# An attention and ReGLU kernel: pair 0's k over a hardware DMA queue instead of GpSimd's

## The chip, the cores and the metric

The kernel runs on one core of a Trainium2 chip. The time is the device time of one execution in microseconds (us); for a version of the kernel it is the median of several runs. One further execution is taken by the hardware profiler, and all times inside the kernel are from that one, counted from the start of its span. The engines are TensorE (PE, with its weight loads as PEld), VectorE (DVE), ScalarE (ACT), GpSimd (POOL) and SyncE (SP). DMAs are issued by SP and ACT over hardware queues, and by GpSimd[...]; only GpSimd's DMAs change the type of the data on the way here (fp32 in HBM to fp16 on the chip).

## What is computed

Eight batches of eight heads, 576 positions, 64 values per head. Each head has two attentions: one over positions averaged in fours, whose result is repeated four times, and one in a band of seven positions. Their sum goes through a gated feed-forward network.

```python
q_d = q.reshape(B, H, Sd, factor, D).mean(axis=3)      # k_d, v_d likewise; factor = 4
out_up = np.repeat(sm_attn(q_d, k_d, v_d), factor, axis=2)
mask = np.abs(pos[:, None] - pos[None, :]) < factor
scores = np.where(mask, scale * np.matmul(q, k.transpose(0, 1, 3, 2)), -1e9)
x = out_up + np.matmul(softmax(scores), v)             # to (4608, 512)
out = (np.maximum(x @ w_gate, 0.0) * (x @ w_val)) @ w_out
```

## The kernel before

The 64 heads are worked off as 32 pairs. For each pair, q, k and v are loaded as fp16 with positions on the partitions: q and k as 96 x 12 x 64 in one slot of a ring of seven (`qk16`), v as 112 x 12 x 64 (`vw`). Then q and k are transposed, so that the 64 values of a head lie on the partitions; pairs from 9 on have this done by DMA transposes and have q and k loaded in two halves each, while the first nine pairs are "flipped" by PE: `emit_flip` (L358) multiplies blocks of q and k by a small constant (an identity beside a matrix that sums fours), and ACT or DVE copy the product out of PSUM into `qkT` and `qkd` (`emit_flipped`, L372). After the flips come the scores (`emit_s1_mm`, L422), exponentials on ACT (`emit_exp`, `emit_ed`), the band mask on DVE (`emit_mask`), and the products with v and pooled v (`emit_s2u`, `emit_s2d`). v is pooled by matmuls with another constant (`emit_vd`, L403). The results are collected, transposed, in `xT`; the feed-forward network takes them in nine chunks of 512 tokens (`emit_h_mm`, L636, and the products with w_out), and the attention of later pairs runs between its matmuls.

Nothing here is scheduled by a compiler: every engine and queue executes in the order in which the program emits. The beginning is the list `FRONT` (L18), a sequence of steps written out by hand, from left to right: `loadk/0` loads pair 0's k, `tr/0/2/4` flips the third part of pair 0 into PSUM bank 4, `ev/0/20V/4` copies it out on DVE (`V`; `A` is ACT), `vd/0/6` pools v, `s1/0/2` are scores, `warm/5/6` are five matmuls on zeros which keep PE busy, `pads` are memsets (`emit_pads`, L279) of the parts of `ee`, `ed`, `vd` and `xo` that no later step writes. PE, for instance, meets pair 0's flips in the order 2, 1, 0, then pools pair 0's v, then runs five matmuls on zeros, and then flips part 0 of pair 1 ahead of pair 0's scores. Of pair 0's flips, part 2 needs k alone, part 1 k and q, part 0 q alone.

Ahead of the list stand (L1097 to L1101):

```python
nc.scalar.dma_start(cst_sb[:, 960:1080], cst_dr[:, 960:1080])
emit_load_q1(0, 0)
nc.sync.dma_start(cst_sb[:, 0:960], cst_dr[:, 0:960])
nc.sync.dma_start(cst_sb[:, 1080:1368], cst_dr[:, 1080:1368])
emit_warm(14, wide=True)
```

The constants are masks and pooling weights (0:960), the flip's constant (960:1080) and one for repeating (1080:1368). Pair 0's q is loaded here by SP in fp32 into `q32`, and ACT casts it into its slot (step `cast`, L1055). All other loads of q, k and v are issued by GpSimd (`emit_load_q1` at L296, `emit_load_v` at L314), one after the other in the order of the list: k and v of pair 0, q, k, v of pair 1, and so on, then slices of the weights. GpSimd's DMAs take eight semaphores in turn, so each waits for the one that was issued eight before it. `gT` (L248) holds the gated hidden layer in two buffers; `gT[1]` is first written by the second chunk of the network.

Of the kernel before, what the change touches and what calls it, by code (L numbers as in the profile page):

```python
# [9 lines left out]
FP32 = mybir.dt.float32  # L10
# [5 lines left out]


FRONT = """  # L18
pads loadk/0 loadv/0 loadq/1 loadk/1 loadv/1 loadq/2 cast tr/0/2/4 loadk/2 ev/0/20V/4 tr/0/1/3
tr/0/0/2 ev/0/21V/4 ev/0/10A/3 vd/0/6 loadv/2 ev/0/11A/3 ev/0/01A/2 ev/0/00A/2 loadq/3 warm/5/6  # L20
tr/1/0/7 vc/0/6 s1/0/2 ev/1/00A/7 loadk/3 tr/1/2/1 ed/0/2 tr/1/1/0 ev/1/20V/1 ev/1/11A/0 loadv/3
sd/0/6 ev/1/21V/1 ev/1/10A/0 rd/0/6 ex/0/0/2 td/0/6 wg/0 vd/1/6 ev/1/01A/7 warm/5/7 ma/0/0
ex/0/1/2 s1/1/0 wv/0 ma/0/1 ed/1/0 ones/4 su/0/4 ex/1/1/0 ru/0/4 loadq/4 ex/1/0/0 tu/0/0/4
# [131 lines left out]
def _dap(t_ap: bass.AP, extra_off: int, dims) -> bass.AP:  # L155
    return bass.AP(tensor=t_ap.tensor, offset=t_ap.offset + extra_off, ap=list(dims))
# [13 lines left out]
def kernel(  # L170
# [10 lines left out]
    nc = tc.nc  # L181
    B, H, S, D = q.shape
# [3 lines left out]
    NB = S // NQ  # L186
    SD = S // 4
# [33 lines left out]
    def ring(n, shape, dtype, name):  # L221
        return [keep.tile(shape, dtype, name=f"{name}{i}") for i in range(n)]
# [5 lines left out]
    qk16 = [t[0:96] for t in qkfull]  # L228
# [7 lines left out]
    ee = ring(2, [WK, 2, S + 32], FP16, "ee_")  # L236
    ed = ring(2, [72, 2, 2 * SD + 64], FP16, "ed_")
    vd = ring(3, [72, 2, 192], FP16, "vd_")
# [7 lines left out]
    q32 = q32full[0:96]  # L246
    r1 = ring(3, [128, TCH], FP16, "r1_")
    gT = ring(2, [128, NJJ, TCH], FP16, "gT_")  # L248
    xT = keep.tile([128, NPB, NTOK], FP16, name="xT")
    ps = psum.tile([128, 8, 512], FP32, name="ps")  # L250

# [24 lines left out]
    for t in qkT:  # L276
        nc.vector.memset(t[:, 2 * S :], 0.0)

    def emit_pads():  # L279
        for t in ee:  # L280
            nc.vector.memset(t[:, :, S:], 0.0)
        for t in ed:
            nc.vector.memset(t[:, :, 2 * SD :], 0.0)
        for t in vd:
            nc.vector.memset(t[:, :, 64:128], 4.0)
        for t in xo:
            nc.vector.memset(t[64:96, NB:, :], 0.0)
# [4 lines left out]
    def head_off(hp):  # L292
        b = (hp // NPB + B0) % B
        return b, (b * H + 2 * (hp % NPB)) * S * D

    def emit_load_q1(hp, i):  # L296

        b, off = head_off(hp)
        src, dst, hh = (q, k)[i // 2], qk16[hp % NL][:, i // 2, :], i % 2
        if hp < NTP:  # L300
            if hh:
                return
            first = hp == 0 and src is q
            (nc.sync if first else nc.gpsimd).dma_start(
                (q32 if first else dst).rearrange("p (n d) -> p n d", d=64),
                _dap(src, off, [[D, 96], [NQ * D, 2 * NB], [1, D]]),
            )
            return
        nc.gpsimd.dma_start(  # L309
            dst.rearrange("p (j h d) -> p j h d", h=2, d=64)[:, :, hh, :],  # L310
            _dap(src, off + hh * S * D, [[D, 96], [NQ * D, NB], [1, D]]),
        )
# [497 lines left out]
    def emit_warm(n, bank=7, wide=False):  # L810
        for _ in range(n):
            nc.tensor.matmul(
                out=ps[:, 7, :] if wide else ps[:, bank, 264:512],
                lhsT=zero_sb[:, 0:128],
                rhs=zero_sb[:, 128 : 640 if wide else 376],
                start=True,
                stop=True,
            )
# [114 lines left out]
    def emit_tail_step(kind, arg, at):  # L933
        c, j = (int(at[0]), int(at[1])) if len(at) == 2 else (int(at or 0), 0)
        i = int(arg[0]) if arg else 0
        if kind in ("hg", "hv"):
            w = int(kind == "hv")
            bank = 4 + i if w else 2 * (j % 2) + i
            emit_h_mm(c, j + NK * i, w, range(4), ps[:, bank, :])
        elif kind == "relu":  # L940
            emit_relu(2 * j + i, ps[:, 2 * (j % 2) + i, :])
        elif kind == "gate":
            emit_gate(c, j + NK * i, 2 * j + i, ps[:, 4 + i, :])
        elif kind in ("gateg", "gateb"):
            nc.vector.scalar_tensor_tensor(
                out=gT[c % 2][:, j + NK * i, :],
                in0=block(c, j, 0).t[i],
                scalar=0.0,
                in1=ps[:, 4 + i, :] if kind == "gateg" else block(c, j, 1).t[i],
                op0=ALU.max,  # L950
                op1=ALU.mult,
            )
        elif kind == "xs":
            emit_xs(c, i)
        elif kind == "wg":
            emit_ws(0, i, 0, 768, nc.vector)
        elif kind == "wv":
            emit_ws(1, i, 192 * int(arg[1]), 192 * int(arg[1]) + 192, nc.gpsimd)
        elif kind in ("qg", "qv"):
            block(c, j, int(kind == "qv")).q(i)  # L960
        elif kind in ("keepg", "keepv"):
            block(c, j, int(kind == "keepv")).keep(i - 1)
        elif kind in ("tg", "tv"):
            block(c, j, int(kind == "tv")).out(arg)
        elif kind == "part":
            lo, hi = ((0, 3), (3, 5), (5, 6))[int(arg[1])]
            unit(c, j).sums(lo, hi, (i,))
        else:
            UNIT_STEPS[kind](unit(c, j), i)

    def emit_step(kind, arg, u, c):

        banks = (u, 1 - u)
        i = int(arg[-1]) if arg and arg[-1].isdigit() else 0
        if kind in H_STEPS:
            pp, jj = banks[i % 2], 6 * u + i
            if kind == "relu":
                emit_relu(i, pair(pp)[:, 0, :])
            elif kind == "gate":
                emit_gate(c, jj, i, pair(pp)[:, 1, :])  # L980
            else:
                w = int(kind == "hv")
                emit_h_mm(c, jj, w, range(4), pair(pp)[:, w, :])
        elif kind in UNIT_STEPS:
            UNIT_STEPS[kind](unit(c - 1, u), i)
        elif kind == "next":
            w = unit(c - 1, 1) if u == 0 else unit(c, 0)
            w.sums(0, NK if u == 0 else 5, (i,))
        else:
            PAIR_STEPS[kind](4 * c + 2 * u + LEAD + "ab".index(arg[0]), arg[1:])  # L990
# [22 lines left out]
    def pool_ab(hp, a):  # L1013
# [15 lines left out]
        "v1": lambda hp, a: emit_v1(hp + 1),  # L1029
        "v2": lambda hp, a: emit_v2(hp + 2),  # L1030
        "qk": ahead(emit_load_q1),
        "v": ahead(emit_load_v),
        "v4": ahead(emit_load_v4),
    }

    def emit_periods(c0, c1):
        for base in range(c0, c1 + 2):
            for tok in ORDER.split():
                c = base + {">": 1, "<": -1}.get(tok[-1], 0)
                kind, arg, u = tok.rstrip("<>").split("/")  # L1040
                if c == c1 - 1 and base > c:
                    continue
                if c0 <= c < c1 or c == c0 - 1 and f"{kind}/{arg}/{u}" in LATE:
                    emit_step(kind, arg, int(u), c)

    def emit_front(tok):
        kind, *a = tok.split("/")
        if "@" in tok:
            emit_step(kind, a[0], *map(int, a[1].split("@")))
        else:  # L1050
            FRONT_STEPS[kind](*[int(x) if x.isdigit() else x for x in a])

    FRONT_STEPS = {
        "pads": emit_pads,
        "cast": lambda: nc.scalar.copy(out=qk16[0][:, 0, :], in_=q32),  # L1055
        "warm": emit_warm,
        "loadq": lambda p: emit_load_q1(p, 0),
        "loadk": lambda p: emit_load_q1(p, 2),
        "loadv": emit_load_v,
        "ones": lambda p: nc.gpsimd.memset(vw[p][:, :, 64:128], 1.0),  # L1060
# [34 lines left out]

    with tc.manual_schedule(engines={ET.PE, ET.DVE, ET.Activation, ET.SP, ET.Pool}):
        nc.scalar.dma_start(cst_sb[:, 960:1080], cst_dr[:, 960:1080])  # L1097
        emit_load_q1(0, 0)
        nc.sync.dma_start(cst_sb[:, 0:960], cst_dr[:, 0:960])
        nc.sync.dma_start(cst_sb[:, 1080:1368], cst_dr[:, 1080:1368])  # L1100
        emit_warm(14, wide=True)  # L1101
        for tok in FRONT.split():
            emit_front(tok)
        emit_periods(PS // 4, (NP - LEAD) // 4)
        for tok in TAIL.split():
            kind, arg, *at = tok.split("/")
            if at:
                emit_tail_step(kind, arg, at[0])
            else:
                emit_step(kind, arg, 1, NCH - 3)  # L1110
# [30 lines left out]
```

## Time and profile before

| | |
|---|---|
| median of five runs | 346.85 us (345.49 to 347.64) |
| profiled execution: its own time, its span | 345.49 us, 343.7 us |
| PE busy, share of the span | 336.4 us, 98% |
| DVE, ACT, POOL busy | 296.7, 218.0, 183.0 us |
| granted clock of PE, mean | 0.999 |
| GpSimd's DMA queue | 132160 packets, 22.63 MB |
| hardware DMA queue of SP | 35632 packets, 16.84 MB |
| PE busy from 0 to 8.2 us, from 8.2 to 24.3 us | 6.74 and 14.26 us (with the matmuls on zeros) |
| PE busy from 24.3 to 60 us | 35.41 of 35.70 us |
| longest wait of PE for a DMA | 0.2 us (0.5 of its weight loads), once |

A matmul counts as busy while it is in the pipeline, so 98% does not mean that PE works at its peak. In the lists below, "SPq" and "ACTq" are DMA issues by SP and ACT[...]. "L304" is a line of the kernel above. In square brackets stands how long the engine had been idle, and what ended that.

### The profile page before, as it was taken

The numbers are of one execution on the slowest core, as the hardware profiler recorded it, in microseconds if no ns is written. First come the engines' busy times: TensorE is split into PE (matmuls) and PEld (weight loads), VectorE is DVE, ScalarE is ACT, GpSimd is POOL, SyncE is SP. The second block draws the span as 40 slices with busy tenths as digits, with TensorE's granted clock in tenths as the row PEclk, the third lists the DMA queues.
The fourth block names the chain that finished last, engine by engine and source line by source line (L and its number), as shares of the span: only waits on it lengthen the run. The fifth ranks groups of instructions, "written<-read, shape, count | busy, mean of one in ns | idle before, by whom it ended". The sixth has DMA issues, their size and how long they took to land.

```text
span 343.7 us, 8266 instructions
## 1 busy us (share of the span) xinstructions
PE 336.4 (98%) x3231; PEld 215.8 (63%) x3231; DVE 296.7 (86%) x546; ACT 218.0 (63%) x423; POOL 183.0 (53%) x232
## 2 busy tenths in 40 slices
PE   8899999999999999999999999999999999999996
PEld 4675556656575656575666556665766557768685
DVE  6694779988999999999999999899999798786892
ACT  4878767767767776677667767776677633334222
POOL 8986557776999796989197777840300000000000
PEclk9999999999999999999999999999999999999999
DMA  9999999999999999999999995992100001001023
GB/s 154 167 170 187 186 190 161 143 168 159 173 145 191 138 188 108 137 162 145 109 108 132 148 162 80 151 154 41 46 16 33 31 2 46 32 31 61 28 67 108
DMA packets 167974, 40.02 MB, mean 116 GB/s; under 512 B 149856, under 2 KB 164864, under 8 KB 167936
## 3 DMA queue, kind: packets, MB, share of 16 engines
q0 software_dynamic: 132160, 22.63, 92.7%
q1 hardware_dynamic: 35632, 16.84, 27.1%
q8 instruction: 25, 0.41, 0.5%
q14 instruction: 13, 0.11, 0.1%
q10 hardware_dynamic: 144, 0.03, 0.1%
HBM read 45.86 MB, written 9.44 MB: 161 GB/s over the span
## 4 chain that ended last, share of the span: by engine, by line
PE 88%; ACT 4%; DVE 3%; DMA 2%; issue 1%; POOL 1%; DVEq 0%; ACTq 0%; POOLq 0%
PE ps L639 47%; PE ps L724 22%; PE ps L905 4%; PE ps L585 3%; PE ps L438 2%; PE ps L427 2%; PE ps L593 2%; PE ps L364 1%; DMA qk<-in_q_dram 1%; PE ps L408 1%; DVE xn L612 1%; ACT rden L603 1%; ACT ed L462 1%; ACT ee L448 1%; DVE xo L718 0%
## 5 line engine op out<-in xcount | busy, mean ns | idle before, releaser
L639 PE MATMUL ps<-xT,wv_sb 128*128 128x512 f16 x432 | 109.0, 379 | 0.0
L639 PE MATMUL ps<-xT,wg_sb 128*128 128x512 f16 x352 | 88.4, 380 | 0.0
L648 ACT ACTIVATE r<-ps 128x512 f16<-128x512 f32 x88 | 52.0, 596 | 31.8 <-PE ps L639 28.9
L639 PEld LDWEIGHTS <-wv_sb 128*128 128x128 f16 x432 | 40.4, 98 | 39.7
L651 DVE TENSOR_TENSOR gT<-r,ps 128x512 f16<-128x512 f16 x88 | 58.9, 680 | 7.0 <-PE ps L639 4.1
L639 PEld LDWEIGHTS <-wg_sb 128*128 128x128 f16 x352 | 32.6, 98 | 32.3 <-issue 0.2
L612 DVE TENSOR_TENSOR xn<-ps,rden 64x720 f16<-64x720 f32 x48 | 43.5, 905 | 4.9 <-ACT rden L608 3.5
L603 ACT ACTIVATE rden<-ps 64x720 f32<-64x720 f32 x48 | 36.7, 765 | 14.2 <-PE ps L593 13.2
L448 ACT ACTIVATE ee<-ps 112x576 f16<-112x576 f32 x64 | 38.7, 647 | 6.2 <-PE ps L438 5.2
L309 POOL DMA_DIRECT2D qk<-in_k_dram x46 | 33.7, 738 | 8.2 <-DMA qk<-in_q_dram 3.6
L309 POOL DMA_DIRECT2D qk<-in_q_dram x46 | 33.7, 737 | 7.9 <-DMA qk<-in_k_dram 4.1
L724 PEld LDWEIGHTS <-gT 128*128 128x128 f16 x324 | 31.5, 98 | 9.0
L454 DVE TENSOR_TENSOR ee<-ee,cst_sb 112x576 f16<-112x576 f16 x64 | 31.6, 514 | 5.2 <-ACT ee L448 4.8
L334 POOL DMA_DIRECT2D vw<-in_v_dram x30 | 28.6, 952 | 8.3 <-PE ps L639 4.9
L724 PEld LDWEIGHTS <-xo 128*128 128x128 f16 x288 | 27.4, 98 | 7.7 <-DVE xo L718 0.3
L351 DVE TENSOR_REDUCE qkd<-qkT 128x288 f16<-128x1152 f16 x23 | 30.9, 1343 | 0.0
L758 ACT COPY q<-ps 128x256 f32<-128x256 f32 x45 | 16.8, 372 | 21.5 <-PE ps L724 21.2
L724 PE MATMUL ps<-wo_sb,gT 128*128 128x256 f16 x216 | 28.0, 273 | 0.0
L724 PE MATMUL ps<-wt,xo 128*128 128x256 f16 x216 | 27.7, 273 | 0.2 <-DVE xo L718 0.2
L386 POOL TENSOR_TENSOR v<-v 72x512 f32<-72x512 f16 x21 | 25.7, 1223 | 2.6 <-DMA v<-in_v_dram 2.0
L571 DVE TENSOR_TENSOR xT<-xn 128x576 f16<-128x576 f16 x28 | 24.1, 861 | 0.5
L915 ACT COPY vw<-ps 128x256 f32<-128x256 f32 x30 | 10.8, 374 | 20.7 <-PE ps L905 13.8
(108 smaller groups left out, 557.5 us busy)
## 6 DMA issues: line engine op xcount, KB each, us to landing
out_dram<-y_sb SPq DMA_DIRECT2D x24, 256.0 KB, 3.8
vw<-in_v_dram POOLq DMA_DIRECT2D x30, 168.0 KB, 7.4
qk<-in_q_dram POOLq DMA_DIRECT2D x46, 72.0 KB, 7.0
qk<-in_k_dram POOLq DMA_DIRECT2D x46, 72.0 KB, 6.7
v<-in_v_dram POOLq DMA_DIRECT2D x21, 144.0 KB, 7.3
out_dram<-y_sb SPq DMA_DIRECT2D x22, 128.0 KB, 1.7
wg_sb<-in_moe_w_gate_dram POOLq DMA_DIRECT2D x4, 384.0 KB, 9.6
wv_sb<-in_moe_w_val_dram POOLq DMA_DIRECT2D x4, 384.0 KB, 10.8
```

Of the source, the lines that this page charges most:

```text
L309: nc.gpsimd.dma_start(dst.rearrange("p (j h d) -> p j h d", h=2, d=64)[:, :, hh, :], _dap(src, off + hh * S * D, [[D, 96], [NQ * D, NB], [ ...
L334: nc.gpsimd.dma_start(t, _dap(v, base, [[D, WK], [NQ * D, n], [1, D]]))
L351: nc.vector.tensor_reduce(out=qkd[hp % 2].rearrange("p i t -> p (i t)"), in_=qkT[hp % 4][:, 0 : 2 * S].rearrange("p (t f) -> p t f", f=4), ...
L386: nc.gpsimd.tensor_tensor(out=m, in0=t[:, :, 0:128], in1=t[:, :, 128:256], op=ALU.add)
L448: nc.scalar.activation(out=o, in_=ps[0:WK, p0 + 2 * g : p0 + 2 * g + 2, 0:288], func=AF.Exp, scale=scale)
L454: nc.vector.tensor_tensor(out=o, in0=o, in1=_sap(masks_sb, (0, WK), 288 * g, [[0, 2], [1, 288]]), op=ALU.mult,)
L603: nc.scalar.activation(out=rden[lo : lo + 64], in_=ps[de : de + 64, 4 + 2 * hh : 6 + 2 * hh, 0:360], func=AF.Ln)
L612: nc.vector.tensor_tensor(out=xn[lo : lo + 64], in0=ps[lo : lo + 64, 4 + 2 * hh : 6 + 2 * hh, 0:360], in1=rden[lo : lo + 64], op=ALU.mult,)
L639: nc.tensor.matmul(out=out, lhsT=w[:, kk, bass.ts(jj, 128)], rhs=xT[:, kk, c * TCH : (c + 1) * TCH], start=(kk == 0), stop=(kk == 3),)
L648: nc.scalar.activation(out=r1[j % 3], in_=h1, func=AF.Relu)
L651: nc.vector.tensor_tensor(out=gT[c % 2][:, jj, :], in0=r1[j % 3], in1=h2, op=ALU.mult)
L724: nc.tensor.matmul(out=out, lhsT=left[:, i, :], rhs=right[i], start=(first and i == 0), stop=(i == NK - 1), skip_group_check=True,)
```

## The change

- `emit_load_q1` sends pair 0's k over SP in fp32, into `k32`, which is a view of the still unused `gT[1]`, and pair 0's q over ACT. k is emitted ahead of q: SP issues k, then its two constants; ACT issues its small constant, then q. GpSimd's first DMA is now pair 0's v, and its list is shorter by one.
- A new step `castk` casts `k32` into pair 0's slot on DVE. In DVE's order it stands after the memsets of `ee` and `ed`, ahead of pair 0's first copies.
- `emit_pads` is split: `pads/0` does `ee` and `ed` where `pads` stood; `pads/1` does `vd` and `xo` after the copies `ev/0/20V` and `ev/0/21V`.
- The first run of matmuls on zeros has 11 instead of 14.

In the order of the engines, these are all of the differences: PE has three matmuls (and their weight loads) less, DVE one cast more, and the six memsets of `vd` and `xo` two copies later, ACT one issue more, GpSimd one issue less, and on SP k stands where q stood. Waits that are new: PE's first flip waits for DVE instead of a GpSimd DMA, pair 0's first pooled product waits for DVE too, and single later instructions wait for the new DMA or the new cast (GpSimd's reload of pair 0's k slot, PE's first read of `gT[1]`, one store of SP). Line numbers grow by 1 to 7 in the changed kernel: L304 becomes L309, L364 becomes L369, L378 L383, the cast of q L1061; the new cast is L1060.

```diff
-pads loadk/0 loadv/0 loadq/1 loadk/1 loadv/1 loadq/2 cast tr/0/2/4 loadk/2 ev/0/20V/4 tr/0/1/3
-tr/0/0/2 ev/0/21V/4 ev/0/10A/3 vd/0/6 loadv/2 ev/0/11A/3 ev/0/01A/2 ev/0/00A/2 loadq/3 warm/5/6
+pads/0 castk loadv/0 loadq/1 loadk/1 loadv/1 loadq/2 cast tr/0/2/4 loadk/2 ev/0/20V/4 tr/0/1/3
+tr/0/0/2 ev/0/21V/4 pads/1 ev/0/10A/3 vd/0/6 loadv/2 ev/0/11A/3 ev/0/01A/2 ev/0/00A/2 loadq/3 warm/5/6
...
+    k32 = gT[1].rearrange("p j t -> p (j t)")[0:96, 0 : 4 * NB * 64].bitcast(FP32)
...
-    def emit_pads():
-        for t in ee:
-            nc.vector.memset(t[:, :, S:], 0.0)
-        for t in ed:
-            nc.vector.memset(t[:, :, 2 * SD :], 0.0)
+    def emit_pads(i):
+        if i == 0:
+            for t in ee:
+                nc.vector.memset(t[:, :, S:], 0.0)
+            for t in ed:
+                nc.vector.memset(t[:, :, 2 * SD :], 0.0)
+            return
         for t in vd:
             nc.vector.memset(t[:, :, 64:128], 4.0)
...
-            first = hp == 0 and src is q
-            (nc.sync if first else nc.gpsimd).dma_start(
-                (q32 if first else dst).rearrange("p (n d) -> p n d", d=64),
+            eng = nc.gpsimd
+            if hp == 0:
+                eng, dst = (nc.scalar, q32) if src is q else (nc.sync, k32)
+            eng.dma_start(
+                dst.rearrange("p (n d) -> p n d", d=64),
...
+        "castk": lambda: nc.vector.tensor_copy(out=qk16[0][:, 1, :], in_=k32),
...
+        emit_load_q1(0, 2)
         emit_load_q1(0, 0)
...
-        emit_warm(14, wide=True)
+        emit_warm(11, wide=True)
```

## The prediction

> **What bounds the kernel now.** I read the page first: TensorE (PE) is busy for 98% of the span, and the row "PEclk" of the forty slices shows a granted clock of 9 tenths or more throughout. So for most of the span the time is set by the stream of matmuls, which this change leaves as it is. It touches the first 9 us, where PE is kept awake with matmuls on zeros and waits for data. The second view is therefore the chain of waits from the start to 9.2 us (start, length, what).
>
> ```profile
> 0.64 0.66 issue
> 1.30 1.04 POOL qk L304
> 2.35 0.92 POOL vw L334
> 3.27 4.89 DMA qk<-in_q_dram
> 8.16 0.04 issue
> 8.21 0.40 PE ps L364 x8
> ...
> 9.15 0.66 ACT ed L462
> ```
>
> GpSimd (POOL) issues pair 0's k, then pair 0's v, then pair 1's q. The chain passes through that third transfer: it lands at 3.27 + 4.89 = 8.16 us, and only then the flips of pair 1 (L364) start. What stands behind them in PE's order (pair 0's scores at 8.54) and in ScalarE's (ACT) order (pair 1's copy at 8.65, then pair 0's exponential at 9.15) goes on from there, through PE, ACT and VectorE (DVE), until PE is full at about 24 us. The view of PE's waits has no wait for a DMA after this one. So the end moves by as much as **pair 1's q** moves, until something else at 8.2 us is later.
>
> The third view tells why the transfer needs 4.89 us for 147 kB (96 x 12 x 64 fp16). It is the busy time by stretches; the last two numbers are the share of the 16 DMA engines (packets overlap, so over 1) and GB/s.
>
> ```profile
> 1.80:2.30 0.50, 0.50 (x3) 0.17 (x2) 0.39 (x2) 0.23 (x1) 0.50 (x1) 1.00 0.76 167
> 2.30:2.80 0.50, 0.50 (x2) 0.15 (x1) 0.50 (x1) 0.00 (x0) 0.50 (x2) 1.00 1.06 202
> 2.80:3.20 0.40, 0.40 (x2) 0.15 (x1) 0.29 (x2) 0.00 (x0) 0.40 (x1) 1.00 1.26 288
> 3.20:4.00 0.80, 0.80 (x3) 0.30 (x2) 0.69 (x2) 0.00 (x0) 0.80 (x2) 1.00 1.10 348
> 4.50:8.20 3.70, 3.51 (x42) 1.95 (x40) 1.99 (x17) 1.76 (x6) 3.70 (x5) 1.00 2.43 155
> ```
>
> From 4.5 us on, the rate is a flat 155 GB/s: GpSimd's transfers follow each other without a gap, one k or q in 147/155 = 0.95 us, one v (172 kB) in 1.11 us. Until then it is the hardware queues' data. The trace's packet records give it by queue: pair 0's q (295 kB in fp32, 1152 packets of 256 B) from 1.80 to 3.54 us, the constants until 4.59 us, and GpSimd's first packet at 3.97 us, although its first issue had ended at 2.34. Thin until the hardware queues run dry: I read it as GpSimd's queue being held by them. Around 59.5 us the records show the same: 34 and 25 packets of GpSimd's queue per half microsecond beside 281 and 327 of the hardware queue, against about 610 when it is alone.
>
> The fourth view is the timeline of the engines up to 7 us, for what the change moves.
>
> ```profile
> 0.75 0.39 SPq L304 DMA_DIRECT2D q<-in_q_dram  x1
> 0.78 0.38 ACTq L1097 DMA_DIRECT2D cst_sb<-cst  x1
> ...
> 4.12 0.83 ACT L1055 CAST qk<-q 96x768 f16<-96x768 f32 x1 [2.10 <-DMA q<-in_q_dram]
> ...
> 4.72 0.19 DVE L283 MEMSET ed<- 72x64 uint32 x2
> 4.88 0.45 DVE L285 MEMSET vd<- 72x128 f16 x3
> 5.39 0.45 DVE L287 MEMSET xo<- 32x128 uint32 x3
> ...
> 6.21 0.67 PEld L364 LDWEIGHTS <-qk 96*64 96x64 f16 x24 [0.42 <-DMA qk<-in_k_dram]
> 6.21 0.82 PE L364 MATMUL ps<-cst_sb,qk 96*64 96x120 f16 x24
> 6.66 0.56 DVE L378 CAST qkT<-ps 128x384 f16<-128x384 f32 x1 [0.82 <-PE ps L364]
> ```
>
> To see here: pair 0's q lands at 4.1 and its cast takes 0.83; DVE has memsets until 5.84; pair 0's flips start at 6.21, when k lands.
>
> **The change part by part.**
>
> *GpSimd's first issue goes* (1.04 us of its time). v of pair 0 is issued at 1.30 instead of 2.33, pair 1's q at about 2.25 instead of 3.27, and everything behind it by 1 us earlier. Counted as issue time alone this is worth -1.04 us at 8.16. But the queue's data, not the issues, are the limit: when q of pair 1 was issued, two transfers were waiting. In data the queue loses k: -0.95 us.
>
> *The same k goes onto the hardware queues* in fp32, 295 kB instead of 147. Everything behind is held longer by X. At the 288 GB/s of 2.80:3.20 X is 1.02 us; at the 202 GB/s of 2.30:2.80, where two rings ran side by side (ACT's small constant beside q), 1.46 us. If a second ring fills what one left idle, so that 1.80 to 2.80 runs at 288 rather than at 167 and 202 (184 kB), 104 kB or 0.36 us are won: X = 0.66. Between these ends I take 1.02, since that row has packets of the same 256 B with the queue in full flow. Sum for pair 1's q: 1.02 - 0.95 = **+0.07 us**, ends 0.66 - 0.95 = -0.29 and 1.46 - 0.95 = +0.51. [...] By the issue rows (1.04) the gain would be a full microsecond[...]. I go with the rates.
>
> *SP and ACT.* k takes q's place on SP (0.75 us), ahead of the two constants; q goes to ACT behind its small constant, at about 1.16. ACT's first packet came 1.48 us after its issue (2.26), SP's 1.05 after, so q begins near 2.7. k should end near 3.6 and land 0.6 later (q: last packet 3.54, cast at 4.12), at 4.2 to 4.4. q ends at 4.3 to 5.0 and lands at 4.9 to 5.6; with 0.83 for the cast it is ready at 5.7 to 6.4. Only the second and third group of pair 0's flips need it; the second runs at 6.48 now. Behind the constants there is the mask, used at 10.9, and the pooling weights, used at 6.97: they should land by 5.8.
>
> *DVE's cast of k*, 96x768 fp32 to fp16, is new. No row has it. From above, DVE's 64x720 product from fp32 takes 905 ns: 0.95 us for 768 columns; from below, the cast from PSUM of half the columns, 0.56. I take 0.56[...]. It begins when the memsets up to ed end, at 4.91, since k is there by then, and ends at 5.47 (or 5.86). Behind it stand the first evictions (6.66 now) and the 0.90 us of the vd and xo memsets, which run after the evictions in DVE's gap up to 9.49; vd's first reader with these columns is the product at 9.85. Nothing waits.
>
> *Three fillers less*: the last warm matmul starts at 5.26 instead of 5.90 and PE is free near 5.5. The clock was released at 4.99 us, before that; price 0. So pair 0's flips start at 5.55 (5.95 with the slow cast) instead of 6.21, and pair 0's evictions end near 7.5 instead of 8.01. That is a gain of 0.5 us in a branch that then waits: PE's next step in order is pair 0's v pooling (v lands at 6.93 + 0.07), five fillers of 0.69, and then the flips of **pair 1**, which wait for its q at 8.16 + 0.07. The cover is that wait; if it went, -0.55 would be the most that could come out.
>
> [...]
>
> *The extra waits* of the new order: PE's first flip waits for DVE's cast (counted above); the product at 9.85 for the vd memsets, done 2 us before; a later reader of the buffer that k borrows, GpSimd's reload of pair 0's slot and one SP store for things done tens of microseconds before: 0.
>
> Sum against the profiled execution: 345.49 (span 343.7 and 1.8 around it) + 0.07 = 345.6. The median of the five runs is 1.36 above that execution, so 346.85 + 0.07 = **346.9 us**: no change.
>
> **Rivals.**
>
> *A (0.52), the sum above*: the microsecond taken from GpSimd's queue is handed to the hardware queues ahead of it. 346.9, own range 346.3 to 347.4. For it: first packet at 3.97, flat 155 GB/s after. That the change doesn't do what it says is part of it: pair 0 flips earlier and nothing follows.
>
> *B (0.22), the queues fill each other's gaps*: the share 0.76 at 1.80:2.30 says that engines were idle, and 3.97 might be GpSimd's own first latency. Then q of pair 1 gains 0.29 at the least, and up to the cap of 0.55 set by pair 0's chain. 346.4.
>
> *C (0.20), slower: two hardware rings share the low rate*. At 202 GB/s or below, with q behind on ACT's ring, GpSimd's first packet comes 1.46 us later, at 5.4, pair 1's q lands at 8.7 and pair 0's own q near 5.6. +0.51: 347.4. It decides from X above 0.95 us; from X = 2.0 it could be measured.
>
> *D (0.06)*: [...]: +0.56, 347.4.
>
> **How the numbers follow.** About 0.3%, or 1.04 us, is what a measurement of this kernel can tell from no change. No case alone reaches it; only their tails and the scatter of the runs (345.49 to 347.64) do. Faster by more: 0.3 of B and a tenth of A, 0.13. Slower by more: nearly half of C, a share of D and a little of A, 0.13. Same: 0.74. The range takes B, C and the scatter of a median: 345.9 to 347.9.
>
> **What would show it.** Right: pair 0's flips start at 5.4 to 6.0; a DVE cast of 0.5 to 0.95 us from 4.9; GpSimd's stretch of 155 GB/s begins about 1 us later, near 5.5 instead of 4.5; pair 1's flips start within 0.3 us of 8.21, still behind their DMA. Wrong: pair 1's flips at 7.7 or earlier (B), at 8.6 or later (C), or a gap in GpSimd's data after the cast (D); a prediction of no change is wrong altogether if the time moves by a microsecond with pair 1's flips in place, for then something after 9 us sets it that I have not seen.

## The result and the profile after

The changed kernel took 349.28 us (median; 346.01 to 355.97), the kernel before 346.68 us beside it on the same chip (344.3 to 348.8): 1.0053 times the time, with an interval of 1.0033 to 1.0073. The forecast of no change, 346.9 us with a range to 347.9, was wrong: the kernel became 0.5% slower. The ratios here leave out executions that lie over 1.5% above the fastest of their kernel; for the changed kernel some of these belong to the effect, as will be seen, so its median moves more (2.6 us, 0.75%) than its ratio.

The executions of the changed kernel fall into groups by their mean granted clock. In 9 of the 23 whose clock is on record (one more than the 22 of the median) it was 0.998 or more (median 347.3 us); in 7 it was about 0.995 (349.5 us); in 7 it was 0.981 to 0.985 (352.0 us). A stretch of 3.41 us at half clock takes 3.41 x 0.5 / 350 = 0.005 from the mean, so these are none, one, and three or four such stretches. The profiled execution is of the last kind: 355.97 us, span 354.2, mean clock 0.981. In the page's forty slices (8.9 us each) it shows at once, in the row of the clock: the first slice at 9, the second at 5, the third at 7.

```profile
PEclk9579999999999999999999999999999999999999
```

The page's row of PE has 9 from the second slice on: PE is busy as before, at half speed (16 flips of pair 0 take 1.01 us at 8.44 below, and 0.61 at full clock in run e2). The view by stretches, cut at the times at which the granted clock changed, gives the place (length; PE, PEld, DVE, ACT, POOL busy; then the clock, the DMA share and GB/s):

```profile
4.22:7.63 3.41, 1.44 (x13) 0.54 (x11) 2.83 (x18) 0.07 (x1) 3.41 (x4) 1.00 1.60 193
7.63:11.05 3.42, 2.61 (x27) 2.01 (x27) 0.00 (x0) 1.91 (x5) 2.81 (x5) 0.50 2.43 155
...
17.87:21.29 3.42, 3.42 (x44) 2.62 (x42) 2.04 (x6) 2.55 (x7) 2.23 (x3) 0.50 1.65 183
```

The full clock was granted at 4.22 us. In the 3.41 us that followed PE was busy for only 1.44 (42%), and at 7.63 the clock was halved, for four times 3.41 us, to 21.29. The kernel before had its clock from 4.99 on, PE busy 3.21 us of the first 3.41 (94%), and kept it:

```profile
4.99:8.40 3.41, 3.21 (x49) 2.00 (x47) 1.50 (x8) 1.50 (x5) 3.41 (x5) 1.00 2.43 155
```

What PE waited for stands in the timeline (start, length, what; the bracket is the idle time before and what ended it):

```profile
4.82 0.64 DVE L1060 CAST qk<-gT 96x768 f16<-96x768 f32 x1
...
5.52 0.40 PE L369 MATMUL ps<-cst_sb,qk 96*64 96x120 f16 x8 [0.27 <-DVE qk L1060]
...
8.44 1.01 PE L369 MATMUL ps<-cst_sb,qk 96*64 96x120 f16 x16 [2.52 <-ACT qk L1061]
```

Pair 0's first flips run on k, at 5.52. The other two thirds wait 2.52 us for ACT's cast of pair 0's **q**. The chain of waits goes through that load, where it went through pair 1's q before:

```profile
1.17 6.36 DMA q<-in_q_dram
7.53 0.02 issue
7.56 0.84 ACT qk L1061
8.40 0.04 issue
8.44 1.01 PE ps L369 x16
9.45 0.75 PE ps L413 x6
10.21 1.03 PE ps L817 x5
11.24 0.54 PE ps L369 x8
```

The last row is pair 1's flips: 11.17 us in the timeline, 8.21 before. The list of DMA issues gives each transfer's time from issue to landing:

```profile
gT<-in_k_dram SPq DMA_DIRECT2D x1, 288.0 KB, 3.6
q<-in_q_dram ACTq DMA_DIRECT2D x1, 288.0 KB, 6.4
cst_sb<-cst SPq DMA_DIRECT2D x1, 240.0 KB, 5.9
```

k, issued at 0.75, lands at 4.4. q, issued at 1.17 on ACT, takes 6.4 us, the constants behind k 5.9. The packet records say how. k's packets run from 1.97 to 3.61 us. ACT's ring (the queue of DMAs that ACT issued) delivers its small constant until 2.48 and q's first packet at 3.13. From 3.68 on come the constants' packets of 1920 B, and q's fall from 181 to 32 per 0.2 us. GpSimd's packets begin at 5.37, though its row for the first issue (POOL, DMA_DIRECT2D) runs from 1.30 to 2.41; the last 64 of q's 1152 end between 5.8 and 7.07, beside both.

How the 10.5 us of the profiled span (354.2 against 343.7) add up is read from ACT's instructions, set beside the same ones before: +3.4 us at the cast of q, +6.1 from 15 to 76 us, +8.0 at 83, +10.6 from 214 to the end. Of the 6.1, 2.96 stand when pair 1's flips start (11.17 - 8.21), and about 1.2 of these are half clock already: from the second flips to pair 1's it is 2.73 us here, and 1.51 at full clock in run e8_14_again below. The other 3.1 come while the clock is half, up to 21.29, and are put down to it. The last 4.5 come in the steady part, at full clock; the kernel before scatters by as much from run to run (344.3 to 348.8), the sums of medians below do not need it, and no run here explains it.

### The profile page after: what moved, and what is told of

Read it like the earlier page. It is cut to its first block, busy times and chain, and to the rows that moved or that the text cites. A ratio compares the mean times of both kernels' runs of the same rounds, so it can differ in the third digit from the quotient of the medians.

```text
span 354.2 us, 8263 instructions
## 1 busy us (share of the span) xinstructions
PE 341.6 (96%) x3228; PEld 219.0 (62%) x3228; DVE 301.2 (85%) x547; ACT 218.4 (62%) x423; POOL 183.2 (52%) x231
## 4 chain that ended last, share of the span: by engine, by line
PE 85%; DVE 9%; ACT 3%; DMA 2%; issue 1%; DVEq 0%; ACTq 0%
PE ps L644 44%; PE ps L729 21%; PE ps L910 4%; PE ps L590 3%; PE ps L369 2%; PE ps L443 2%; DVE ee L459 2%; PE ps L432 2%; DVE xo L723 2%; DVE gT L656 2%; DMA q<-in_q_dram 2%; DVE xn L617 2%; PE ps L598 1%; PE ps L413 1%; PE ps L817 1%
## 5 line engine op out<-in xcount | busy, mean ns | idle before, releaser
L459 DVE TENSOR_TENSOR ee<-ee,cst_sb 112x576 f16<-112x576 f16 x64 | 32.5, 528 | 5.7 <-ACT ee L453 5.2
L391 POOL TENSOR_TENSOR v<-v 72x512 f32<-72x512 f16 x21 | 26.9, 1280 | 1.4 <-DMA v<-in_v_dram 0.8
L576 DVE TENSOR_TENSOR xT<-xn 128x576 f16<-128x576 f16 x28 | 25.8, 923 | 0.5
## 6 DMA issues: line engine op xcount, KB each, us to landing
wv_sb<-in_moe_w_val_dram POOLq DMA_DIRECT2D x4, 384.0 KB, 10.5
```

Source lines behind the costliest of these rows:

```text
L391: nc.gpsimd.tensor_tensor(out=m, in0=t[:, :, 0:128], in1=t[:, :, 128:256], op=ALU.add)
L459: nc.vector.tensor_tensor(out=o, in0=o, in1=_sap(masks_sb, (0, WK), 288 * g, [[0, 2], [1, 288]]), op=ALU.mult,)
```

## The experiments

Three accounts were tried against each other. The theory: q's late landing leaves PE idle between its first and second flips, and the clock is lost for it. Rivals: it is GpSimd's queue, held longer by the larger hardware data, that delays pair 1's q and all after it; or it is the three matmuls on zeros that are missing, whatever the loads do. In the texts that stood before the runs the theory is T1, in the third batch T2; the rivals are R1 (the queue) and R2 (the fillers, that is the matmuls on zeros). Runs are named below by the first part of their name, as a1 or e2. Each batch ran on one chip, beside the kernel before (346.46, 346.91 and 346.04 us), which by its mean clock lost a window itself in 9 of 68, 2 of 59 and 5 of 40 executions.

**The first batch.** The changed kernel once more, with no edit:

> The changed kernel once more, to see how much pair 0's q varies from one profile to the next. T1 (q on ScalarE's ring comes behind the constants on SyncE's, PE then stands idle for 2.5 us and its clock is halved for one to four windows of 3.4 us): q's last packet again later than 6 us, PE's second group of flips near 8 us, several executions with a mean clock of 0.985 to 0.995, time 348 to 352. R1 (too much hardware data ahead of GpSimd's queue, wherever q stands): GpSimd's queue at full rate again only from 7 us.

349.15 us, 1.0069 [1.0044, 1.0093]. In the profile q's last packet came at 6.09, PE idled 2.02 us, the window around it was 41% busy, and the clock was halved from 8.16 to 11.57. So the loss repeats, with one window instead of four. By the mean clock 8 of 15 executions lost it; the other seven took 348.1 us, 1.7 above the kernel before, where the first measurement had 0.6.

q on SP, behind k and ahead of the constants:

```
-                eng, dst = (nc.scalar, q32) if src is q else (nc.sync, k32)
+                eng, dst = nc.sync, (q32 if src is q else k32)
```

> Pair 0's q goes to SyncE, behind k and ahead of the constants; all else as changed. T1: q's last packet near 4.6 us, lands near 5.2, its cast ends near 6.0, PE idles less than 0.5 us before the second group of flips, no execution with the clock below 0.998, time 346.0 to 347.3 (q of pair 1 as forecast, near 8.2). R1: q early too, but GpSimd's queue at full rate only from about 7, pair 1's flips 1 to 1.6 us late, time 347.7 to 348.3 with the clock untouched. R2 (three fillers less let the clock go): the clock drops as in the changed kernel, 349 or more.

348.25 us, 1.0056 [1.0035, 1.0077]: a miss for the theory, which wanted 346 to 347.3 and no loss of clock. q's last packet came at 5.02 as hoped, and PE idled only 0.75 us before the second flips (6.81). But now the constants were last (7.04 and 7.77), pair 0's v pooling waited for them until 7.59, and in the profiled execution the clock was still halved from 12.01 to 15.42, after a window (8.60 to 12.01) with PE busy for 66%. So the gap at q is not the only weak place of this front. The time lies in the range that R1 gave (347.7 to 348.3), but R1 wanted pair 1's flips 1 to 1.6 us late and the clock untouched: they are 0.66 late (8.87), and 10 of 22 executions lost a window. Twelve executions of 348.1 us with a mean clock of 1.0 stay unexplained (see the last batch for one possible reason).

Twelve matmuls on zeros put into the gap:

```
-pads/0 castk loadv/0 ... cast tr/0/2/4 loadk/2 ev/0/20V/4 tr/0/1/3
+pads/0 castk loadv/0 ... cast tr/0/2/4 warm/12/6 loadk/2 ev/0/20V/4 tr/0/1/3
```

> Twelve matmuls on zeros (248 columns, about 1.3 us) between the first and the second group of pair 0's flips; all else as changed, so q is as late. T1: the 3.4 us window after 4.2 us is then busy for about nine tenths, the clock stays at 1.0 in all or nearly all executions, and what is left is the delay of q alone: about 347.3, as in those executions of the changed kernel that kept their clock, up to 349.7 if the whole 3 us of the profile carry through. R2: same direction. R1: the clock is by the way, time unchanged at 349.3.

347.2 us, 1.0011 [0.9993, 1.0028], and the clock was kept in all 22 executions. The timeline of its PE shows the fillers ahead of the second flips, which start without a wait:

```profile
6.46 1.44 PE L817 MATMUL ps<-zero_sb 128*128 128x248 f16 x12
7.83 0.61 PE L369 MATMUL ps<-cst_sb,qk 96*64 96x120 f16 x16
```

q is as late as before this edit (last packet 5.89, a1 6.09), and so are the other loads: pair 1's q was issued at 2.38 and took 6.3 us, in a1 2.40 and 6.2. Only the idleness is gone, and most of the loss with it. That speaks against the rival of GpSimd's queue.

The two large constants moved to ACT, behind q:

```
-        nc.sync.dma_start(cst_sb[:, 0:960], cst_dr[:, 0:960])
-        nc.sync.dma_start(cst_sb[:, 1080:1368], cst_dr[:, 1080:1368])
+        nc.scalar.dma_start(cst_sb[:, 0:960], cst_dr[:, 0:960])
+        nc.scalar.dma_start(cst_sb[:, 1080:1368], cst_dr[:, 1080:1368])
```

> The two larger constants are issued by ScalarE behind q instead of by SyncE behind k; SyncE has k alone. T1 in the form that the constants on the other ring are what q waits for: q's last packet near 4.5 us, landing near 5.1, no clock loss, 346.3 to 347.5. If k's ring or GpSimd's queue holds q instead: q's last packet still after 5.5 us and the clock drops as before. R1: 347.7 to 348.3 from pair 1's q, clock at 1.0.

347.49 us, 1.0027 [1.001, 1.0043]. q's last packet came at 5.20 instead of 6.09, so the constants on SP's ring had cost it about 0.9 us (one profile each); PE idled 0.42 us there. Nine executions of 22 still lost one window by their mean clock, one three or more. More than half of the loss of a1 went. The time came out as the theory had it, at the upper end (346.3 to 347.5); q (near 4.5) and the clock (no loss) did not.

**The second batch: each half of the change alone.** q by ACT, everything else as before:

```
-            (nc.sync if first else nc.gpsimd).dma_start(
+            (nc.scalar if first else nc.gpsimd).dma_start(
```

> The kernel before with one thing changed: pair 0's q is issued by ScalarE instead of SyncE (k stays with GpSimd, 14 fillers). T1: q again stands behind SyncE's constants for a part, so that it ends near 4.3 to 4.8 us instead of 3.54, but the hardware queues have no more data than before, so GpSimd's queue starts where it did; k lands at about 6.2, q is cast before that, nothing is late: 346.0 to 347.0, clock kept as in the kernel before. If ScalarE's ring alone were the fault (whatever the amount of data): q's last packet after 5.5 us, PE idle before the second group, clock losses, 348 or more.

346.44 us, 0.9994 [0.997, 1.0019]; clock kept in all 12. q's last packet came at 4.64. Here the constants went first on SP (the larger until 3.19; q's first packet at 3.08), but k was not there. ACT's ring alone cost nothing here.

The rest alone: the loads as before, but 11 matmuls on zeros and the split memsets:

```
-        emit_warm(14, wide=True)
+        emit_warm(11, wide=True)
```

> The rest of the change alone: memsets split, 11 fillers instead of 14, all loads as before. T1: PE idles from 5.5 to 6.2 us and then goes on as before; at most the odd execution loses its clock, 346.3 to 347.2. R2 (the fillers are what loses the clock): half of the executions with a mean clock of 0.985 to 0.995, 348 or more.

346.81 us, 0.9997 [0.9968, 1.0026]; 9 of 12 kept the clock, 3 lost one window (2 of 59 of the kernel before). So fewer fillers may let the clock go more often, at no cost in time that this run can show. The profile has a gap too, before the first flips:

```profile
7.00 0.82 PE L367 MATMUL ps<-cst_sb,qk 96*64 96x120 f16 x24 [1.61 <-DMA qk<-in_k_dram]
```

A gap of 1.61 us with all 24 flips behind it was not long enough here. So the second rival falls in its plain form (it wanted 348 or more): three fillers less cost nothing measurable with the loads of before. It survives as half of the cause, by the next run. The changed kernel with 14 matmuls on zeros:

```
-        emit_warm(11, wide=True)
+        emit_warm(14, wide=True)
```

> The changed kernel with 14 fillers again. T1: they shorten the idle time of PE ahead of q's cast by about 0.6 us of 2 to 2.5, q is as late, the clock still drops in a good part of the executions, 348 to 349. R2: the clock is kept and the time is back at 346.5 to 347.2.

346.74 us, 1.0002 [0.9984, 1.0021]; 19 of 20 kept the clock. The gap was 1.15 us (6.87 to 8.02). This is what R2 wanted; the theory had put it at 348 to 349, and missed. With the loads of the change, the three fillers decide.

The kernel before with less on the hardware queues, to try the step on GpSimd's queue: two of the masks moved to GpSimd, behind pair 1's v and pair 2's k.

```
-        nc.sync.dma_start(cst_sb[:, 0:960], cst_dr[:, 0:960])
-        nc.sync.dma_start(cst_sb[:, 1080:1368], cst_dr[:, 1080:1368])
+        nc.sync.dma_start(cst_sb[:, 576:960], cst_dr[:, 576:960])
...
+        "masks": lambda: nc.gpsimd.dma_start(cst_sb[:, 0:576], cst_dr[:, 0:576]),
+        "rep4": lambda: nc.gpsimd.dma_start(cst_sb[:, 1080:1368], cst_dr[:, 1080:1368]),
```

> The opposite of the change, at the kernel before: 221 kB of constants (masks and the repeating matrix, first used after 10 us) leave SyncE's queue and come over GpSimd's, behind pair 1's v and pair 2's k; SyncE has q and the pooling weights alone. T1 with hardware data first and GpSimd's queue after it: GpSimd's queue at full rate about 0.5 to 0.7 us earlier (near 3.9 instead of 4.5), pair 1's flips at about 7.6 instead of 8.21 unless another wait takes over, time about 0.4 below before: 346.0 to 346.4. If GpSimd's first packet comes when its own software is ready: first packet still at 3.97, no change, 346.5 or, with the masks late, more.

346.96 us, 1.0014 [0.9992, 1.0037]. GpSimd's first packet came at 3.52 instead of 3.97, and in the changed kernel at 5.37. The amount of hardware data alone does not set it, though: e1, with as much as the changed kernel, had 4.22, and e4, with as much as the kernel before, 4.23. The flips did not come earlier (pair 0's at 7.24, pair 1's at 8.96), and nor did the end. In this execution the clock was first granted at 7.07, so the 14 fillers ran to 7.31, where before they ended at 6.28, and the flips waited for PE:

```profile
1.26 6.05 PE L812 MATMUL ps<-zero_sb 128*128 128x512 f16 x14 [1.26 <-DVE zero_sb L271]
```

Inconclusive on the size of the step.

**The third batch: the number of fillers, for and against the clock.** The changed kernel again, with its 11:

> The changed kernel (11 fillers) on the same chip as the next three, so that the fillers are compared beside each other. T2 (new: q's lateness opens a gap in PE's work ahead of the second group of flips, and the three fillers less make it long enough for the clock's window; neither alone does it): clock lost in a third to two thirds of the executions, 348 to 349.5. If the 14-filler run was clean only because of its chip: this one is clean as well, 346.7 to 347.3.

349.83 us, 1.0057 [1.0023, 1.009]; 5 of 14 kept the clock (346.7 us), 4 lost one window (349.6), 5 three or more (352.7). Its profile is like the first: q's last packet at 7.10, a window 23% busy, half clock from 8.80 to 19.04, and this wait:

```profile
9.08 1.01 PE L369 MATMUL ps<-cst_sb,qk 96*64 96x120 f16 x16 [2.92 <-ACT qk L1061]
```

The changed kernel with 14 again, the same edit as above:

> The changed kernel with 14 fillers, again, beside the one with 11. T2: clock lost in at most a tenth of the executions, 346.5 to 347.3, clearly below the run with 11. If the chip was the reason: as the run with 11.

347.35 us, 1.0034 [1.0012, 1.0056]; clock kept in all 9. It took back 2.5 us of 349.83, but here not all: 1.3 us stay, where the second batch had none left. The chain of waits shows a delay at full clock:

```profile
1.19 5.63 DMA q<-in_q_dram
...
7.73 0.61 PE ps L369 x16
8.34 0.44 PE ps L413 x6
8.78 0.53 PE ps L817 x5
9.31 0.33 PE ps L369 x8
```

The late q of pair 0 delays pair 1's flips (9.24 against 8.21), through PE's order: second flips, pooling of v, five fillers, then pair 1. Pair 1's own q had landed by 8.6 (issued at 2.40, 6.2 us). ACT's instructions lie 1.03 us later at the front, as this chain says. But this is not shown to be the 1.3 us. In e6, the same kernel at 1.0002, pair 1's flips start later still, and in e4, e5 and e7, all near 1, they start at 8.77 to 8.96:

```profile
9.53 0.40 PE L369 MATMUL ps<-cst_sb,qk 96*64 96x120 f16 x8
```

The changed kernel with 8:

```
-        emit_warm(11, wide=True)
+        emit_warm(8, wide=True)
```

> The changed kernel with 8 fillers. T2: the gap is longer still, the clock is lost in more executions than with 11, three or more windows in most, 350 to 352. If the number of fillers does not matter: as with 11.

352.15 us, 1.0126 [1.0083, 1.017]. In the profile, taken of an execution of 348.2 us, PE idled 0.66 and 1.85 us, and the full clock was first granted at 12.56. And the kernel before with 8:

```
-        emit_warm(14, wide=True)
+        emit_warm(8, wide=True)
```

> The kernel before with 8 fillers instead of 14: PE idles from about 4.7 to 6.2 us, with q and k where they were. T2: a gap of 1.5 us and then dense work: lost clock in under a third of the executions, 346.7 to 348. R2 in its strong form (the fillers alone decide, whatever q does): as the changed kernel with 8.

348.47 us, 1.0055 [1.0032, 1.0079], more than the theory's 346.7 to 348 and far from what R2's strong form wanted, the 352.15 of the changed kernel. So the loads of before lose the clock too, with a gap long enough: PE idled 1.92 us for k, and the full clock was first granted at 19.29. This shows a trap in reading. First its row in the view of the cores, then its flips in the timeline:

```profile
core 0: 348.0 us, clock 0.999
```

```profile
6.77 1.41 PE L364 MATMUL ps<-cst_sb,qk 96*64 96x120 f16 x24 [1.92 <-DMA qk<-in_k_dram]
```

The mean clock is 0.999, although the same 24 flips took 1.41 us instead of 0.82. The rows count only from the first time the clock is granted, and read 1.00 before (in the first profile for 0 to 4.20 us as well, with the grant at 4.22). An execution that gets its clock late thus looks undisturbed: by the mean, five executions of the changed kernel with 8 fillers "kept" it and took 352.3 us; of the kernel before with 8, fifteen "kept" it and took 349.75, five lost one window and took 347.5. Some of those sorted as undisturbed above, e1's twelve and a1's seven among them, may be of this kind. The length of a well known matmul tells it; the column does not.

Together, as ratios to the kernel before:

| matmuls on zeros | loads of before | loads of the change |
|---|---|---|
| 14 | 1 | 1.0002 and 1.0034 |
| 11 | 0.9997 | 1.0053, 1.0069 and 1.0057 |
| 8 | 1.0055 | 1.0126 |

## Why the prediction was wrong

**Shown: the loads and the missing fillers cost 0.5 to 0.7% together, and most of it goes when PE has no gap.** The fillers alone cost nothing that was seen (0.9997), the loads alone nothing on one chip and 0.3% on another (1.0002 and 1.0034). The loads leave PE without work until q is there. With three fillers less the first flips start 0.7 to 1.1 us earlier (5.52 to 5.76 with 11, 6.47 and 6.58 with 14) while q is as late, and in over half of the executions the clock is lost for one to four windows. With matmuls in the gap and q as late, e2 kept the clock in all executions and took 347.2 us where a1 took 349.15 and the kernel before 346.46: about 2.0 of the 2.7 us went.

The groups of the first measurement seem to say it too: one lost window 349.5 - 347.3 = 2.2 us, three or four 4.7. This is not the price of the clock alone. A window at half speed can hold PE back by at most 3.41/2 = 1.7 us (an estimate that halves all of PE's work), and the executions that lose the clock may be those in which q is latest. In e1 those with one lost window were no slower than those with none (348.1 both, though some of the latter may have been granted it late), in e3 by 0.2 us.

By the prediction's steps:

- **"The clock was released at 4.99 us, before that; price 0"** is the step that failed most. It treated the clock as won once and for all, and its time as fixed. In the profiles of this study it was granted at 4.2 to 7.1 us with 11 or 14 fillers, different in each; whatever came later came at multiples of 3.41 us after it. After windows with PE busy for 23, 41 and 42% it was halved, once after 66% (e1); e5 kept it after 52%, e6 after 66%. So no sharp threshold comes out of these views. Where the price stood at 0, keeping PE busy took back 2.0 us (e2), and the three fillers 2.5 (a3 to e8). The gap before the second flips does not tell it by itself: it was 2.5, 2.0 and 2.9 us in the first profile, a1 and a3, each shorter than a step of 3.41 us. Together with the thin work around it these are the profiles of the 42, 41 and 23%; the forecast made no such sum.
- **q of pair 0, "lands at 4.9 to 5.6", ready at 5.7 to 6.4.** Measured: last packet 5.9 to 6.2 in five executions and 7.1 in two, where 4.3 to 5.0 stood; cast done at 7.7 to 9.0. The term counted k and q and left out the constants, which SP issues at 1.21 and 1.86 on the other ring. With them it is 295 + 246 + 74 + 31 + 295 = 941 kB, from 1.80 us on at the 288 to 202 GB/s that the prediction had: 5.1 to 6.5 us. The upper end was in reach. e3 puts the constants' share at 0.9 us; e1 and e4 show that neither k ahead nor the constants alone would have done it (5.02, 4.64). q also began later than the 2.7 of the forecast, at 3.0 to 3.5 with the new loads, after its ring's small constant (through at 2.5 to 3.2). How the engines divide themselves between the queues no run shows. Measured in the first profile: q's packets of 256 B fell from 181 to 32 per 0.2 us beside the constants' of 1920 B, rose to 87, and were 5 to 15 from 5.8 to 7.0, beside about 100 to 230 of GpSimd's. The constants are not all of it: in a3 they were through at 6.37, and q's last 40 packets came after that, up to 7.10, beside GpSimd's alone (about 230 per 0.2 us). So the constants seem to delay q into GpSimd's queue, which then holds it too; no run separates the two.
- **"Only the second and third group of pair 0's flips need it"** was true and led to the wrong end. PE takes its list in order (second flips, pooling, fillers and pair 1's flips at 8.44, 9.45, 10.21 and 11.24 in the first chain), so pair 0's second group stands ahead of everything that the chain goes through. The branch was called covered up to 8.2 us without setting q's upper end against it: 6.4 for the cast, 0.61 for the flips, 0.44 for the pooling and 0.53 for the fillers left 0.2 us. With the cast done at 7.7 this is what e8's chain shows, and its +1.03 us at the front.
- **Pair 1's q, +0.07 us with ends -0.29 and +0.51.** Not settled. It landed at 8.6 to 9.0 in seven profiles with the new loads, at 9.8 and 10.1 in the two with the latest q. The forecast set it against the 8.16 of one profile; with pair 0's k still on GpSimd's queue it landed at 8.1 in e7, but at 8.8 or 8.9 in e4, e5 and e10. So +0.07 lies within the scatter from one profile to the next, and so does the upper end. GpSimd's first packet came at 5.37, as rival C had it, and its 155 GB/s began near 7.0 (6.0 in a1), not 5.5. Rival C had the right place (two rings, a late q of pair 0) and a price that followed the wrong transfer: 0.51 us through pair 1's q, nothing through PE's idleness.
- **Right:** the first flips start at 5.52 in the first profile; the cast of k takes 0.62 to 0.65 us from 4.82 (0.56 was taken; the upper end, 905 ns x 768/720, is 0.97, not 0.95) and delays nobody; the moved memsets, at 6.66 and 7.17, cost nothing. Nor did GpSimd slow down at the cast: its two issues beside it took 0.96 us (a v, whose mean was 0.95 before) and 0.91 (a q, others at the front 0.88 and 0.89), and behind it its packets rise without the gap of rival D, from about 20 to about 245 per 0.2 us between 5.4 and 7.4.

Left open: why single executions gain or lose 1 to 4 us after 80 us; why 14 fillers left 1.3 us on one chip and none on another; and how many executions were granted the clock late, since only profiled ones tell. No variant beat the kernel before.

## What to carry to other kernels

When a change moves work at the start, count PE's busy share in each 3.41 us around it (the step of the clock in these profiles), with every wait at its upper end, and treat matmuls on zeros as part of that sum: here three of them, with no measurable effect under one order of loads, were worth 2.5 us of 350 under another. Read the landing of a load from several profiles before you build on it: pair 1's q scattered by 0.7 us with the loads of before. When a load moves to a second ring, set against it all bytes of the other ring, also those issued later: here q's last packet came 0.9 us earlier when two constants left SP's ring (6.09 in a1, 5.20 in e3). And follow an in-order engine's list past the late operand, not only that operand's own readers: in e8 pair 1's flips started at 9.24 instead of 8.21, in a chain that goes through a q they do not read.

## What the runs showed of the hardware

- In these profiles the clock changes only in steps of 3.41 us, counted from its first grant. A lost clock came back after windows with PE busy for all of their time (a1, a3, e1 and the first profile), not after 76, 91 and 86% (the first profile). One full window was not enough in e10: the one below was not followed by the grant, which came two windows later.

```profile
9.05:12.47 3.42, 3.42 (x50) 2.46 (x49) 0.51 (x2) 1.61 (x4) 3.42 (x5) 1.00 2.44 155
```

- The first grant followed windows, counted back from it, with PE busy for 87% or more in every profile. With eight fillers PE was busy without a break only from 1.26 to 4.86; the window that held most of it was busy for 81% (e9, 2.32 to 5.74) and 77% (e10, 2.23 to 5.64), and the grant did not come.
- So it came late, at 12.56 and 19.29 us, with eight fillers, while the mean clock in the profile reads 1.0.
- In the first profile the second hardware ring delivered its first packet of q 2.0 us after its issue, behind the ring's small constant; k's came 1.2 us after its own (1.97 for 0.75).
